# A gated MLP behind an RWKV recurrence: sequence parts of 256 tokens in place of halves of 384

## The chip, the core and the metric

The kernel runs on one core of a Trainium2 chip. TensorE (PE) multiplies, VectorE (DVE), ScalarE (ACT) and GpSimd (POOL) do the element-wise work, and SyncE (SP) issues the transfers. The metric is the device time of one execution in microseconds, as the median of several executions.

## What is computed

Four sequences of 768 tokens, 8 heads of width 48, go through a recurrence; its output, 384 wide, goes through a gated MLP that also mixes along the sequence.

```python
for t in range(S):                                     # S = 768
    cur = einsum('bhd,bhe->bhde', u[None] * kt, vt)
    y[:, :, t] = einsum('bhd,bhde->bhe', rt, state + cur)
    state = wt[..., None] * state + einsum('bhd,bhe->bhde', kt, vt)
x = y.transpose(0, 2, 1, 3).reshape(B, S, 384)
h = gelu(x @ w_in)                                     # 384 -> 1024
u, v = h[..., :512], h[..., 512:]
v_n = (v - mean(v)) / sqrt(var(v) + 1e-6) * g_ln
v_s = einsum('ts,bsd->btd', w_sg, v_n) + b_sg[None, :, None]
out = x + (u * v_s) @ w_out                            # 512 -> 384
```

The weights of w_in and w_out arrive as 64-bit numbers.

## The kernel before

The recurrence is cut into 24 chunks of 128 tokens (6 for each of the 4 sequences), called steps. A step loads decays, keys, receptances and values, scans the decays on VectorE (`decays`), and then needs PE for many products of 64x64 (`scores`, `products`, `outputs`; from the seventh step on these are one piece, `stretch`). VectorE puts the masked scores in place (`masked`, L776) before a step's outputs can be made, and forms the states between (`state`, `decayed`). A step leaves its output in the PSUM tile `y_ps` as four turned blocks of 128 columns. `taken` copies them to SBUF: two blocks and one block to `x`, the fourth to `y3`, from where three small transfers per step or half (`move`) bring rows of heads 3 and 7 into `x`. `split_x` splits `x` into two fp32r numbers, a high part `xh` and the rest `xl`.

The MLP works on halves of a sequence, `HALF` = 384 tokens (three steps). Each product of two fp32 matrices is made as three fp32r products, high by high, high by low, low by high (`mm3_part`, L976 to L978). There are four kinds of pieces, and each gathers in one PSUM bank (`m_ps`, three banks, and `resets`, a fourth from the eighth step on):

- `v_piece`, one per step (24): 9 products of 512 columns. ACT takes the GELU, ACT, POOL and DVE normalise and split the result into `vn`.
- `u_piece`, 4 per half: 9 products of 384 columns, then a GELU on ACT (L1032).
- `gate_piece`, 4 per half: 18 products of 384 columns over all six `vn` of the sequence, then a chain DVE (L1054), DVE (L1056), ACT (L1058), DVE (L1060) that leaves the gated tile `g` and frees the bank.
- `out_piece`, 3 per half: 12 products of 384 columns over the half's four `g`, an add on DVE (L1078) into one of two tiles `o`, and a transfer to `out`. The very last one is cut into two of 192 columns.

So there are 216 products of 512 columns, 1140 of 384 and 24 of 192. The sequence weights w_sg come in as 6 loads of 384 KB and are split in `f32_weight`.

A planner (`Plan`) writes the order of every engine's instructions when the program is built: each piece is a generator that yields one operation after the other with the engines it may go to, and what is next is chosen by ranks (`LEAD`, `FIRST`, `PIECE`, `WEIGHT`, `SHIFT`, `AHEAD`) and by the planner's own costs. The engines then run these orders strictly in sequence. Gaps of PE that the planner sees early in the program are filled with products that nobody reads (`warm`, L510).

Of the kernel before, what the change touches and what calls it, by code (L numbers as in the profile page):

```python
# [29 lines left out]
HALF = S // 2  # L30
NB = 2 * NP
# [5 lines left out]
LEAD = (11.6025, 5.98611, 1.71578, -0.150446)  # L37
FIRST = {"v": -3.83166, "u": 19.8393, "gate": 1.89446, "out": 11.2319}
PIECE = {"v": -2.4207, "u": 7.13579, "gate": 9.59843, "out": -5.81453}
WEIGHT = {"v": -11.5804, "u": -32.1839, "sg0": 28.8303, "sg1": -2.3904, "out": -5.37898}  # L40

BIAS = {"DVE": 0.305835, "POOL": 0.124508}
TOL = {"ACT": 0.0369713, "DVE": 0.040863, "PE": 0.0432678, "POOL": 0.0667837, "SP": 0.02}
OWN = {"ACT": 0.12, "DVE": 0.12, "PE": 0.0, "POOL": 0.1}
SHIFT = {
    "f64_weight": {3: -0.0614381, 4: 0.171028, 7: -1.58436, 8: 0.20308, 9: 1.30876},
    "f64_check": {0: -0.0471499, 1: 0.159946, 3: 0.257724, 4: 0.297904, 5: 0.297904, 6: 0.297904, 7: -0.0975631,
        8: 0.0401798, 9: 1.01451},
    "range_check": {1: -0.671107, 4: -0.273385, 5: -0.692899, 6: -1.18207, 7: 0.365565, 8: 0.257825, 9: -7.61137,
        11: -0.201453},  # L50
    "f32_weight": {0: 0.266801, 1: 0.266801, 2: 1.2626, 3: 0.777485, 4: 0.777485, 5: 0.406698},
    "columns": {0: 1.52176},
    "consts": {0: 1.1105},
    "load_v": {0: 0.477108, 2: 0.231396, 3: 0.0395037, 4: -0.138812, 5: -0.736247, 6: -1.71658, 7: -0.736247,
        8: -0.736247, 9: -0.0362696, 10: -0.620509, 11: 0.110577, 12: 0.251922, 13: 0.533938, 14: 0.0194044,
# [12 lines left out]
    "decayed": {0: -1.48561, 3: 0.136849, 4: 0.0768776, 8: -1.85101, 9: 0.25626, 13: -0.520287, 14: -0.520287,
        15: -0.520287, 16: -0.520287, 17: -0.520287, 18: -0.520287, 19: -0.0972287},
    "outputs": {1: 0.014777, 2: -1.0276, 3: 0.123273, 4: 0.123273, 5: 0.531604},  # L70
    "decays": {2: 0.0537525, 3: 0.104777, 4: -0.706109, 8: 0.360113, 11: 0.0881192, 13: 0.435941, 15: 0.223668,
        18: -1.17132, 19: 0.0148464, 20: -0.0367773, 21: 0.0148464, 23: -0.0570478},
    "masked": {2: -1.53943, 3: 0.373784, 5: -5.29511, 7: 0.0206628, 9: 0.973368, 11: 0.387743, 12: 2.10614,
        13: -2.29062, 15: -0.0676852, 17: -0.805431, 18: -0.805431},
    "taken": {2: -1.13338, 3: -0.0634019, 7: -0.898706, 11: -1.06242, 14: -0.384535, 15: -3.82209, 16: -0.589404,
        17: 0.771624, 18: -0.12312, 19: 0.0250502, 21: 4.68329, 22: 0.138749, 23: 0.0264215},
    "load_w": {4: -0.131786, 5: 0.0401692, 6: 0.0401692, 7: -0.121604, 8: 0.0401692, 9: -0.164737, 10: -0.0704624,
        12: 0.188933, 13: 0.0377871, 15: 0.902008, 17: 0.289032, 18: -0.0123312, 20: -0.246017, 21: -1.39921,
        22: 0.915889, 23: 10.1272},
    "load_rk": {0: -0.685585, 8: -0.0367111, 9: -0.0654356, 10: -0.0654356, 11: -0.0654356, 12: -0.328397,  # L80
        13: 0.156304, 14: -0.0654356, 15: -0.99069, 17: 0.197626, 18: 0.0344045, 19: 0.0344045},
    "load_kr": {6: 0.0701331, 7: -0.328212, 8: 0.0701331, 9: 0.0701331, 11: 0.123607, 13: -1.42981, 14: -1.42981,
        15: -1.42981, 18: 0.450623, 19: 0.569158, 20: 0.569158, 21: 0.118535, 22: 0.337379},
    "stretch": {0: -0.014311, 1: 3.71987, 2: -0.0649968, 3: -0.305745, 4: -0.0196869, 7: 5.17364, 9: 0.181751,
        10: 0.0035684, 11: 2.497, 12: 0.0035684, 13: 0.263689, 15: 0.0334773, 16: 0.583982},
    "chunk_pc": {7: -3.79915, 8: -2.65237, 9: -3.8422, 10: 0.110729, 19: -0.652345, 20: 0.179569, 22: 3.75926,
        23: -0.146839},
    "turned_copy": {2: -2.70266, 3: 2.36122, 5: 0.715675, 6: -3.03549, 7: 0.715675, 9: -0.172946, 10: -0.287854,
        11: -2.02959, 15: -0.298449},
    "move": {0: 1.40363, 1: -0.0424312, 2: 0.162164, 3: -0.0424312, 5: -0.771782, 6: 0.514385, 7: 0.0471732,  # L90
        8: 0.84335, 9: 0.319766, 10: 0.657144, 11: 0.040942},
    "split_x": {0: 0.10165, 1: -0.157134, 3: -3.17149, 4: -0.0132548, 5: -0.112868, 6: -0.112868, 7: 11.4787,
        8: -0.180189, 9: -9.43369, 10: 4.40471, 11: 5.72521, 12: 12.8962, 13: 0.0052103, 18: 0.523091, 21: 1.51135,
        22: 0.815484, 23: 1.22284},
    "v_piece": {1: 0.44266, 4: 0.117358, 7: 0.0515489, 8: 0.0515489, 13: -0.241269, 14: 0.172728, 15: 0.172728,
        19: -1.50804, 22: -8.36947, 23: 1.91087},
    "gate_piece": {0: 0.0381263, 2: -1.34922, 3: -0.0424933, 4: -2.33629, 8: -4.06543, 9: -4.20633, 10: -4.20633,
        11: -4.20633, 12: -4.20633, 19: 0.103656, 21: -0.533896, 25: -0.154439, 26: -2.39311, 27: -0.644318,
        28: -0.644318},
    "out_piece": {0: -5.63328, 2: -0.0987209, 3: 0.17867, 7: 3.7878, 8: 0.328413, 9: 0.328413, 10: 0.328413,  # L100
        11: 0.42777, 12: 0.42777, 13: 0.0993568, 14: 0.0993568, 15: -2.84073, 16: 3.05659, 17: -0.0251354,
        19: -0.134011, 20: 0.199046, 22: 5.16223, 23: -0.367422, 24: -2.24201},
    "u_piece": {4: 6.46487, 5: 6.1215, 6: 4.75292, 7: 5.03861, 8: 4.53855, 9: 1.98717, 11: 0.120666, 14: -0.26405,
# [294 lines left out]
def rwkv_gmlp(ctx: ExitStack, tc: tile.TileContext, wpad, kr, vtok, ktok, vt, u, ucol, w_in, consts_, w_sgT, w_out, out):  # L398
# [502 lines left out]
    def taken(n):  # L901
# [529 lines left out]
```

## Time and profile before

| | |
|---|---|
| median of 3 executions | 362.49 us (362.28 to 363.86) |
| the profiled execution, its own time | 362.22 us |
| span in its profile | 360.5 us |
| PE busy | 349.4 us, 97% of the span |
| DVE busy | 270.1 us, 75% |
| ACT busy | 201.9 us, 56% |
| POOL busy | 96.5 us, 27% |
| PE clock granted | 0.997 of full speed |
| moved by DMA | 57.06 MB, mean 158 GB/s |

The span is what the profiler records on the core; the rest of an execution's own time, 1.7 us here, lies around it. Busy shares are means over the span: PE runs through all of it, DVE is near full in the first 200 us and a third busy afterwards, when only MLP pieces are left. A product's row in the profile gives how long it is under way, from its start to the modelled end. Consecutive products overlap, so the pace of PE is read from start to start.

### The profile page before, as it was taken

Reading aid. Unit: us, or ns where it says so; the run is one execution under the profiler, and the core shown is the slowest. Engines: PE = TensorE matmul, PEld = TensorE weight load, DVE = VectorE, ACT = ScalarE, POOL = GpSimd, SP = SyncE. Lnnn points to the kernel's source line nnn. Section 1 sums busy time; section 2 is a strip of 40 time slices with the busy share of each in tenths; the row PEclk is TensorE's granted clock in tenths of the full one; section 3 lists DMA queues with packets and bytes.
Section 4 is the critical chain, followed back from the end, with each engine's and each line's share of the span. In section 5 each row is a group of like instructions: output and inputs, shape, how many; then the busy total and the mean of one; then the engine's idle time right before and its main releaser. Section 6 shows DMA issues by size and latency. Waiting matters only on the chain.

```text
span 360.5 us, 10959 instructions
## 1 busy us (share of the span) xinstructions
PE 349.4 (97%) x4507; PEld 321.5 (89%) x4507; DVE 270.1 (75%) x555; ACT 201.9 (56%) x526; POOL 96.5 (27%) x158
## 2 busy tenths in 40 slices
PE   7999999999999999999999999989999999999992
PEld 7887688899999899899999899879998989999991
DVE  6999999999999989988999979638322545362341
ACT  2847797852534655753343455835267999991110
POOL 7234444214044422226432132223000024200000
PEclk9999999999999999999999999999999999999998
DMA  7969987512448627533664234123546935521001
GB/s 249 368 197 364 318 280 233 158 32 76 162 140 254 191 82 236 171 124 122 189 220 152 79 95 139 43 82 98 163 140 202 308 99 175 188 60 65 2 11 63
DMA packets 26697, 57.06 MB, mean 158 GB/s; under 512 B 3216, under 2 KB 12176, under 8 KB 26640
## 3 DMA queue, kind: packets, MB, share of 16 engines
q1 hardware_dynamic: 26640, 56.29, 48.5%
q8 instruction: 37, 0.61, 0.7%
q14 instruction: 20, 0.16, 0.1%
HBM read 50.37 MB, written 4.72 MB: 153 GB/s over the span
## 4 chain that ended last, share of the span: by engine, by line
PE 90%; DMA 4%; POOL 2%; SPq 1%; issue 1%; DVE 0%; DVEq 0%; POOLq 0%
PE m_ps L976 18%; PE m_ps L977 18%; PE m_ps L978 18%; PE resets L976 6%; PE resets L977 5%; PE resets L978 5%; PE a_ps L699 5%; PE y_ps L722 4%; PE y_ps L733 3%; PE y_ps L706 2%; DMA RK<-in_ktok 2%; DMA x<-y 2%; PE m_ps L510 1%; PE a_ps L706 1%; DMA out<-o 1%; PE m_ps L965 1%
## 5 line engine op out<-in xcount | busy, mean ns | idle before, releaser
L976 PE MATMUL m_ps<-wsgh,vn 128*128 128x384 f32 x138 | 47.1, 341 | 0.0
L977 PE MATMUL m_ps<-wsgl,vn 128*128 128x384 f32 x138 | 46.6, 338 | 0.0
L978 PE MATMUL m_ps<-wsgh,vn 128*128 128x384 f32 x138 | 46.6, 338 | 0.0
L1007 POOL TENSOR_TENSOR st<-st,mhalf 128x1 f32<-128x1 f32 x24 | 14.0, 582 | 67.6 <-DVE st L1005 34.8
L976 PE MATMUL m_ps<-xT,winh 128*128 128x384 f32 x78 | 27.1, 348 | 0.0
L977 PE MATMUL m_ps<-xT,winh 128*128 128x384 f32 x78 | 26.4, 339 | 0.0
L978 PE MATMUL m_ps<-xT,winl 128*128 128x384 f32 x78 | 26.4, 338 | 0.0
L976 PEld LDWEIGHTS m_ps<-wsgh,vn 128*128 128x128 f32 x138 | 25.9, 188 | 0.5
L977 PEld LDWEIGHTS m_ps<-wsgl,vn 128*128 128x128 f32 x138 | 25.9, 188 | 0.2
L978 PEld LDWEIGHTS m_ps<-wsgh,vn 128*128 128x128 f32 x138 | 25.9, 188 | 0.0
L976 PE MATMUL m_ps<-g,wouth 128*128 128x384 f32 (+1 forms) x76 | 25.7, 339 | 0.0
L977 PE MATMUL m_ps<-g,wouth 128*128 128x384 f32 (+1 forms) x76 | 25.5, 335 | 0.0
L978 PE MATMUL m_ps<-g,woutl 128*128 128x384 f32 (+1 forms) x76 | 25.5, 335 | 0.0
L1054 DVE SCALAR_TENSOR_TENSOR m_ps<-m_ps,flat 128x384 f32<-128x384 f32 x23 | 14.2, 621 | 14.9 <-PE m_ps L978 14.7
L1058 ACT CAST g<-m_ps 128x384 fp32r<-128x384 f32 x23 | 10.9, 477 | 24.9 <-DVE m_ps L1056 24.9
L663 POOL TENSOR_TENSOR RK<-RK,flat 128x384 f32<-128x384 f32 x15 | 15.2, 1012 | 35.7 <-DVE W L609 11.8
L976 PE MATMUL m_ps<-winh,xT 128*128 128x512 f32 x60 | 24.7, 411 | 0.0
L978 PE MATMUL m_ps<-winh,xT 128*128 128x512 f32 x60 | 23.7, 396 | 0.0
L977 PE MATMUL m_ps<-winl,xT 128*128 128x512 f32 x60 | 23.7, 396 | 0.0
L1032 ACT ACTIVATE u<-m_ps 128x384 f32<-128x384 f32 x26 | 12.7, 493 | 19.5 <-PE m_ps L978 19.5
L405 ACT COPY x<-y_ps 128x256 f32<-128x256 f32 (+1 forms) x39 | 11.2, 328 | 22.0 <-PE y_ps L722 16.6
L722 PE MATMUL y_ps<-a,vtok 64*64 64x64 f32 x768 | 21.6, 224 | 1.3 <-issue 1.2
(194 smaller groups left out, 1031.6 us busy)
## 6 DMA issues: line engine op xcount, KB each, us to landing
KR<-in_kr SPq DMA_DIRECT2D x24, 512.0 KB, 4.8
RK<-in_ktok SPq DMA_DIRECT2D x20, 384.0 KB, 3.6
W<-in_wpad SPq DMA_DIRECT2D x24, 260.5 KB, 3.3
KR<-in_wpad SPq DMA_DIRECT2D x12, 521.0 KB, 4.4
vtok<-in_vtok SPq DMA_DIRECT2D x24, 192.0 KB, 3.3
out<-o SPq DMA_DIRECT2D x23, 192.0 KB, 2.5
vn<-in_w_in SPq DMA_DIRECT2D x6, 512.0 KB, 5.6
KR<-in_w_in SPq DMA_DIRECT2D x6, 512.0 KB, 4.1
```

What stands on the lines that cost most here:

```text
L405: nc.scalar.copy(o, i) if e == "ACT" else engine[e].tensor_copy(o, i)
L663: engine[op.e].tensor_tensor(t[:, 0], t[:, 0], u_bc, ALU.mult)
L699: nc.tensor.matmul(ps_[64 * c_:64 * c_ + 64, j, p * C:p * C + (2 * T if c_ < turn else T)], x.K[rows, at:at + T], r_, start=True, stop=True)
L706: m = behind(m, nc.tensor.matmul(at(c_)[64 * j:64 * j + 64, p // 2, p % 2], x.kt.tile[64 * c_:64 * c_ + 64, j, p * 64:(p + 1) * 64], x.V[6 ...
L722: m = nc.tensor.matmul(place(y, j, q, r, c_), x.V[64 * c_:64 * c_ + 64, h * D - up(p, j):h * D - up(p, j) + 64], x.a.tile[64 * c_:64 * c_ ...
L976: nc.tensor.matmul(ps, lh, rh, start=(i == 0), stop=False)
L977: nc.tensor.matmul(ps, lh, rl, start=False, stop=False)
L978: nc.tensor.matmul(ps, ll, rh, start=False, stop=(i == n - 1))
L1007: nc.gpsimd.tensor_tensor(rstd, var, c.mhalf, ALU.pow)
L1032: nc.scalar.activation(h_.u[f].tile, ps, AF.Gelu_apprx_tanh)
L1054: nc.vector.scalar_tensor_tensor(ps, ps, c.g[:, d:d + 1], c.b_bc[:, ts], ALU.mult, ALU.add)
L1058: nc.scalar.copy(gh, ps)
```

## The change

The MLP works on three parts of 256 tokens (`PARTS` = 3, `PART` = 256, two steps each) in place of two halves of 384.

- All fp32r products have 256 columns: u, gate and out pieces become 12 instead of 8 sets, each piece with as many products as before; a `v_piece` makes its 512 columns as two products of 256 side by side in one bank. That is 2160 products: 432 for v, 432 for u, 864 for gates, 432 for outputs.
- `taken` copies three of the four blocks in one instruction, so a step has two copies instead of three.
- The tiles for `x`, `xT`, `u`, `g` and `o` are 256 wide; there are 5, 3, 12, 4 and 2 of them (3, 2, 8, 4 and 2 before).
- The outputs of the last part go into free `u` tiles instead of the two `o` tiles, and the last output piece is no longer cut in two.
- w_sg comes as 9 loads of 256 KB.
- All ranks of the planner and its costs for the changed pieces are new, and so is the order on every engine.

```diff
+GP = 2
+PART = GP * C
+PARTS = S // PART
-LEAD = (11.6025, 5.98611, 1.71578, -0.150446)
+LEAD = (6.61435, 3.0082, 1.07907, -0.0504834)
...
-    s_x = slots("x", 3, [KT, HALF])
+    s_x = slots("x", 5, [KT, PART])
-    s_xt = homes("xT", 2)
+    s_xt = homes("xT", 3)
-    s_u = slots("u", 8, [HALF])
+    s_u = slots("u", 12, [PART])
-    s_o = slots("o", 2, [HALF])
+    s_o = slots("o", 2, [PART])
...
     def taken(n):
-        y0, y1 = (y.tile[:, j, :, 0:C] for j in range(2))
+        three = y.tile.rearrange("p j q t -> p (j q) t")[:, 0:3, 0:C]
-        copy(op.e, half.x.tile[:, 0:2, cs], y0)
-        op = yield Op({"ACT": 0.19, "DVE": 0.22}, free=[y], apart=True)
-        copy(op.e, half.x.tile[:, 2, cs], y1[:, 0])
+        copy(op.e, half.x.tile[:, :, cs], three)
         op = yield Op({"ACT": 0.19, "DVE": 0.22}, take=[s_y3] if first else [], free=[y], apart=True)
-        copy(op.e, half.y3.tile[:, cs], y1[:, 1])
+        copy(op.e, half.y3.tile[:, cs], y.tile[:, 1, 1, 0:C])
...
     def v_piece(b, g):
         for k in range(KT):
-            mm3_part(m.tile, ((xh[:, k, cs], xl[:, k, cs]),
-                              (c.win_h[:, k, FF:2 * FF], c.win_l[:, k, FF:2 * FF])), k, KT)
+            for i in range(2):
+                at, fs = (slice(o + i * FF // 2, o + (i + 1) * FF // 2) for o in (0, FF))
+                mm3_part(m.tile[:, at], ((xh[:, k, cs], xl[:, k, cs]), (c.win_h[:, k, fs], c.win_l[:, k, fs])), k, KT,
+                         i == 0, False)
...
     def u_piece(b, half, f):
-            ps = m.tile[:, :HALF]
+            ps = m.tile[:, :PART]
     def gate_piece(b, half, d):
-        ds, ts = slice(d * 128, d * 128 + 128), slice(half * HALF, (half + 1) * HALF)
+        ds, ts = slice(d * 128, d * 128 + 128), slice(half * PART, (half + 1) * PART)
-            ps = m.tile[:, :HALF]
+            ps = m.tile[:, :PART]
...
-    def out_piece(b, half, i, k=0, parts=1):
+    def out_piece(b, half, i):
-        op = yield Op({"DVE": 0.06 + 0.42 / parts}, take=[s_o], free=[m, h_.x])
+        op = yield Op({"DVE": 0.33}, take=[s_u if (b, half) == (B - 1, PARTS - 1) else s_o], free=[m, h_.x])
-        nc.vector.tensor_tensor(o.tile[:, 0:w], ps, h_.x.tile[:, i, at], ALU.add)
-        yield dma(192 // parts, free=[o])
+        nc.vector.tensor_tensor(o.tile, ps, h_.x.tile[:, i], ALU.add)
+        yield dma(128, free=[o])
...
     def f32_weight(src, hi, lo, done, after):
-        op = yield dma(384, take=[s_g], slack=2.0, after=after)
+        op = yield dma(256, take=[s_g], slack=2.0, after=after)
```

Three places show what the new order does. The first is the end of the program on VectorE: in both the rows begin with the last gate (`bad` is a one-element result that is ready there), and the rows that write `o` or `u` are the last output adds. Before:

```order
L1054 SCALAR_TENSOR_TENSOR m_ps_0_132<-m_ps_0_132,flat 128x384
L1102 TENSOR_SCALAR bad<-m_ps_0_133 1x1
L1056 TENSOR_TENSOR m_ps_0_132<-m_ps_0_132,u_0_120 128x384
L1060 TENSOR_TENSOR g_4508<-m_ps_0_132,g_4508 128x384
L1078 TENSOR_TENSOR o_0_129<-resets,x_0_111 128x192
L1078 TENSOR_TENSOR o_0_128<-m_ps_0_134,x_0_111 128x192
L1078 TENSOR_TENSOR o_0_129<-m_ps_0_133,x_0_111 128x384
L1078 TENSOR_TENSOR o_0_128<-m_ps_0_132,x_0_111 128x384
```

With the change, at the same place on VectorE:

```order
L1087 SCALAR_TENSOR_TENSOR m_ps_0_138<-m_ps_0_138,flat 128x256
L1133 TENSOR_SCALAR bad<-resets 1x1
L1089 TENSOR_TENSOR m_ps_0_138<-m_ps_0_138,u_0_130 128x256
L1093 TENSOR_TENSOR g_5457<-m_ps_0_138,g_5457 128x256
L1109 TENSOR_TENSOR u_0_121<-m_ps_0_140,x_0_111 128x256
L1109 TENSOR_TENSOR u_0_122<-m_ps_0_139,x_0_111 128x256
L1109 TENSOR_TENSOR u_0_127<-resets,x_0_111 128x256
```

Four adds that take turns in two tiles have become three adds in three tiles. The second place is PE shortly after its last gate piece: the first products of the last outputs that read the last gate tile, which is `g_4508` before and `g_5457` with the change. Before:

```order
L976 MATMUL m_ps_0_133<-g_4464,wouth 128x384
L977 MATMUL m_ps_0_133<-g_4464,wouth 128x384
L978 MATMUL m_ps_0_133<-g_4464,woutl 128x384
L976 MATMUL resets<-g_4508,wouth 128x192
L977 MATMUL resets<-g_4508,wouth 128x192
L978 MATMUL resets<-g_4508,woutl 128x192
```

With the change, on PE:

```order
L1007 MATMUL m_ps_0_139<-g_5436,wouth 128x256
L1008 MATMUL m_ps_0_139<-g_5436,wouth 128x256
L1009 MATMUL m_ps_0_139<-g_5436,woutl 128x256
L1007 MATMUL m_ps_0_140<-g_5457,wouth 128x256
L1008 MATMUL m_ps_0_140<-g_5457,wouth 128x256
L1009 MATMUL m_ps_0_140<-g_5457,woutl 128x256
```

Between the last product of the last gate and the first one that reads its tile, PE had 18 products of 192 columns and 6 of 384; now it has 18 of 256. The third place is SP's queue at about 22 us, where the first step's output rows (`x<-y`) go out among the loads; `g<-in_w_sgT` are the loads of w_sg and `RK<-in_ktok` those of a step's keys and receptances. Before:

```order
L568 DMA KR_0_83<-in_kr 128x1024
L1168 DMA g_456<-in_w_sgT 128x2x384
L582 DMA RK_0_90<-in_ktok 128x768
L1168 DMA g_488<-in_w_sgT 128x2x384
L1168 DMA g_499<-in_w_sgT 128x2x384
L582 DMA RK_0_91<-in_ktok 128x768
L576 DMA vtok_0_88<-in_vtok 128x384
L568 DMA KR_0_84<-in_kr 128x1024
L944 DMA x_0_110<-y_0_113 32x128 x3
```

With the change, on SP:

```order
L974 DMA x_0_110<-y_0_115 32x128
L615 DMA RK_0_90<-in_ktok 128x768
L615 DMA RK_0_91<-in_ktok 128x768
L1199 DMA g_505<-in_w_sgT 128x2x256
L1199 DMA g_524<-in_w_sgT 128x2x256
L1199 DMA g_532<-in_w_sgT 128x2x256
L592 DMA W_0_81<-in_wpad 128x521
L609 DMA vtok_0_88<-in_vtok 128x384
L601 DMA KR_0_84<-in_kr 128x1024
L974 DMA x_0_110<-y_0_115 32x128 x3
```

One load of 512 KB (`KR_0_83`) has gone ahead of the first step's rows, the three loads of w_sg between the first and the second step's rows are a third smaller, and a load of the decays (`W_0_81`) has come in between.

More of the change, by code (lines that the diff above doesn't have):

```diff
@@ L34 @@
 WMID, WHALF = 1.11, 0.48
-LEAD = (11.6025, 5.98611, 1.71578, -0.150446)
[L38 to L43, printed above, removed]
+LEAD = (6.61435, 3.0082, 1.07907, -0.0504834)
+FIRST = {"v": 0.538535, "u": 10.0542, "gate": 8.23501, "out": 1.251}
@@ L44 @@
+PIECE = {"v": -32.3005, "u": 3.53526, "gate": 6.48944, "out": -13.6143}
+WEIGHT = {"v": -7.69722, "u": -28.2188, "sg0": -18.159, "sg1": 0.318838, "sg2": -1.30212, "out": -26.9792}
+BIAS = {"DVE": 0.430508, "POOL": 0.254095}
+TOL = {"ACT": 0.108412, "DVE": 0.0272938, "PE": 0.107725, "POOL": 0.0671664, "SP": 0.02}
 OWN = {"ACT": 0.12, "DVE": 0.12, "PE": 0.0, "POOL": 0.1}
 SHIFT = {
-    "f64_weight": {3: -0.0614381, 4: 0.171028, 7: -1.58436, 8: 0.20308, 9: 1.30876},
-    "f64_check": {0: -0.0471499, 1: 0.159946, 3: 0.257724, 4: 0.297904, 5: 0.297904, 6: 0.297904, 7: -0.0975631,
-        8: 0.0401798, 9: 1.01451},
@@ L650, in own_weights @@
             engine[op.e].tensor_tensor(t, x.K, x.R, ALU.mult)
-            op = yield Op({"PE": 0.8}, small=True, after=[e_uc], take=[m_m], free=[rk], n=16)
+            op = yield Op({"PE": 1.0}, small=True, after=[e_uc], take=[m_m], free=[rk], n=16)
             m, = op.got
@@ L904, in taken @@
         x = ch[n]
-        half = halves[b, g // 3]
-        first = g % 3 == 0
-        cs = slice((g % 3) * C, (g % 3) * C + C)
-        op = yield Op({"ACT": 0.3, "DVE": 0.35}, after=[x.e_ym], take=[s_x] if first else [], apart=True)
+        half = halves[b, g // GP]
+        first = g % GP == 0
+        cs = slice((g % GP) * C, (g % GP) * C + C)
+        op = yield Op({"ACT": 0.42, "DVE": 0.47}, after=[x.e_ym], take=[s_x] if first else [], apart=True)
         y = x.y
-        y0, y1 = (y.tile[:, j, :, 0:C] for j in range(2))
+        three = y.tile.rearrange("p j q t -> p (j q) t")[:, 0:3, 0:C]
         y.done(op.seen)
@@ L1041, in gate_piece @@
                 first += e_wout
-            op = yield Op({"PE": 0.53}, after=[s_.e_v[s], e_wsg[s, half], *first], take=[] if s else [m_m, s_g],
+            op = yield Op({"PE": 0.347}, after=[s_.e_v[s], e_wsg[s, half], *first], take=[] if s else [m_m, s_g],
                           done=h_.e_gm[d] if s == NC - 1 else None)
@@ L1049, in gate_piece @@
             vn.done(op.seen)
-        yield Op({"DVE": 0.54}, after=[e_u, h_.e_u[d]])
-        g.n = KT + ((b, half) == (B - 1, 1))
-        g.new(2, HALF, dtype=F32R)
+        yield Op({"DVE": 0.37}, after=[e_u, h_.e_u[d]])
+        g.n = KT
+        g.new(2, PART, dtype=F32R)
         gh = g.tile[:, 0]
         nc.vector.scalar_tensor_tensor(ps, ps, c.g[:, d:d + 1], c.b_bc[:, ts], ALU.mult, ALU.add)
-        yield Op({"DVE": 0.5}, free=[h_.u[d]])
+        yield Op({"DVE": 0.35}, free=[h_.u[d]])
@@ L1082, in verdict @@
+        yield dma(128, free=[o])
+        nc.sync.dma_start(out[b, ms, half * PART:(half + 1) * PART], o.tile)
     def verdict():
@@ L1105, in rwkv_gmlp @@
     e_win = [[Event() for _ in range(KT)] for _ in range(2)]
[L1106 removed]
+    e_wsg = {(s, i): Event() for s in range(NC) for i in range(PARTS)}
     e_wout = [Event() for _ in range(FT)]
@@ L1228, in rwkv_gmlp @@
     for b in range(B):
-        for i in range(2):
+        for i in range(PARTS):
             h_ = halves[b, i]
@@ L1245, in rwkv_gmlp @@
             for m in range(KT):
-                parts = 2 if (b, i, m) == (B - 1, 1, KT - 1) else 1
-                for k in range(parts):
-                    plan.add(h_.n + at["out"] + 0.1 * m + 0.01 * k, out_piece(b, i, m, k, parts))
+                plan.add(h_.n + at["out"] + 0.1 * m, out_piece(b, i, m))
     plan.add(50.0, verdict())
```

240 lines of the change are left out of this document (128 added, 112 removed), and 13 rows, old and new, of the table SHIFT.

## The prediction

> **What bounds the kernel now.** I read three views in this order: the chain of work that ended last, what PE waited for, and the busy time of each engine by stage. The chain gives each step's share of the span; the list of PE's waits, here from 60 us on, gives engine, line, releaser, total us, times and the longest; the stages give busy us and, in brackets, instructions.
>
> ```profile
> PE 90%; DMA 4%; POOL 2%; SPq 1%; issue 1%; DVE 0%; DVEq 0%; POOLq 0%
> ```
>
> ```profile
> PE y_ps L722 <- issue: 1.2, 1, 1.2
> PE y_ps L706 <- issue: 0.2, 1, 0.2
> ```
>
> ```profile
> core 0: us, PE busy (x) PEld busy (x) DVE busy (x) ACT busy (x) POOL busy (x), PEclk, DMA share, GB/s
> 0.00:45.00 45.00, 42.58 (x674) 33.86 (x674) 41.04 (x85) 26.78 (x80) 20.63 (x49) 1.00 0.86 300
> 60.00:100.00 40.00, 40.00 (x405) 37.55 (x404) 39.51 (x86) 23.06 (x66) 9.29 (x14) 1.00 0.38 118
> 100.00:200.00 100.00, 100.00 (x1636) 94.34 (x1635) 92.26 (x177) 48.72 (x144) 36.83 (x43) 1.00 0.56 173
> 300.00:353.50 53.50, 53.42 (x309) 52.41 (x307) 23.96 (x53) 27.63 (x50) 4.56 (x8) 1.00 0.25 77
> 353.50:360.50 7.00, 0.00 (x0) 0.00 (x0) 0.56 (x1) 0.00 (x0) 0.00 (x0) 0.85 0.19 64
> ```
>
> PE carries 90% of the chain, and after the start-up it waits for next to nothing: 1.4 us in 300, and that for no other engine ("issue"). From 60 to 200 us it has no idle time at all, at the full granted clock, although DVE is nearly full beside it (131.8 of 140 us). In the first 45 us PE, DVE and DMA (0.86, 300 GB/s) share the bound, and the last 7 us belong to the end of the output. So the time is PE's work, plus the start-up, plus the end. A busy PE is not yet the pace of PE, since products overlap; the pace is read from start to start, in the timeline (start, us under way, line, tiles, shape):
>
> ```profile
> 281.08 0.34 PE L976 MATMUL m_ps<-wsgh,vn 128*128 128x384 f32 x1
> ...
> 282.47 0.34 PE L978 MATMUL m_ps<-wsgh,vn 128*128 128x384 f32 x1
> 300.13 0.34 PE L977 MATMUL m_ps<-g,wouth 128*128 128x384 f32 x1
> ...
> 301.89 0.34 PE L978 MATMUL m_ps<-g,woutl 128*128 128x384 f32 x1
> 304.19 0.39 PE L976 MATMUL m_ps<-winh,xT 128*128 128x512 f32 x1
> ...
> 305.82 0.40 PE L977 MATMUL m_ps<-winl,xT 128*128 128x512 f32 x1
> ```
>
> ```profile
> 349.50 0.27 PE L977 MATMUL resets<-g,wouth 128*128 128x192 f32 x1
> ...
> 350.06 0.36 PE L976 MATMUL m_ps<-g,wouth 128*128 128x384 f32 x1
> 7.42 0.97 PEld L655 LDWEIGHTS m_ps<-u_col,RK 128*128 128x128 f32 x8
> ```
>
> The 384-wide pace is 0.1738 us here for gates (8 products from 281.08 to 282.47) and 0.1760 for outputs (10 from 300.13 to 301.89). The 512-wide one is 0.2329 (7 from 304.19). The 192-wide one is 0.112 (5 from 349.50). The last row shows eight weight loads of 128 columns in 0.97 us under products of only 8 columns; one load is under way for 0.19, so they follow each other every 0.111. A product of 192 columns therefore pays for its weights, while those of 384 and 512 pay for their columns, at 0.453 to 0.458 ns a column.
>
> **The products, part by part.** Before, 1140 x 0.176 + 216 x 0.2329 + 24 x 0.112 = 200.6 + 50.3 + 2.7 = 253.6 us. Afterwards there are 2160 products of 256 columns, which no row shows. The columns are the same, 552,960; twice as many as need be would only hurt if a product fell under the floor of its weights. From below the bound is that floor, 0.112. From above it is the line through 384 (0.1760) and 512 (0.2329), 0.0569 for 128 columns, so 0.1760 - 0.0569 = 0.1191. By the column, 256 x 0.453 to 0.458 is 0.116 to 0.1173. I take 0.1165: the rows by the column are the nearest, and it lies in the middle of them, between the two ends. That makes 251.6 us, **2.0 us less** than before, with bounds of 241.9 (11.7 less) and 257.3 (3.7 more).
>
> [...]
>
> **The evictions on DVE and ACT.** These rows give the count, then ns as min/median/max, first and last start, and shapes:
>
> ```profile
> L1054 DVE SCALAR_TENSOR_TENSOR m_ps<-m_ps,flat x23: 609/625/627, 85.8 to 346.2; 128x384 f32<-128x384 f32 x23
> L1056 DVE TENSOR_TENSOR m_ps<-m_ps,u x23: 548/566/567, 86.9 to 346.9; 128x384 f32<-128x384 f32 x23
> L1060 DVE TENSOR_TENSOR g<-m_ps,g x23: 532/548/558, 88.4 to 348.0; 128x384 fp32r<-128x384 f32 x23
> L1078 DVE TENSOR_TENSOR o<-m_ps,x x19: 357/557/558, 105.6 to 354.5; 128x384 f32<-128x384 f32 x18, 128x192 f32<-128x192 f32 x1
> ```
>
> ```profile
> L405 ACT COPY x<-y_ps x39: 265/372/375, 21.1 to 278.0; 128x256 f32<-128x256 f32 x22, 128x128 f32<-128x128 f32 x17
> ```
>
> An add of 192 columns takes 357 ns and one of 384 takes 557, so 192 columns are worth 200 ns and the rest is fixed: 128 columns less save 0.13 us. A gate's three DVE instructions fall from 1.74 us to 1.35, but there are 48 gates instead of 32: 64.8 us for 55.6. Output adds go from 23 x 0.557 + 2 x 0.357 = 13.5 us to 36 x 0.424 = 15.3. So DVE gains 11.0 us of work. On ACT one more block costs 0.1 us, so the merged copy of three blocks costs 0.47 for 0.37 + 0.27 in two, 0.17 less for each of 24 steps, some 4 us. These 11.0 us on DVE cost the span nothing as long as PE finds its next step ready. Before, at the twentieth step, the masked scores are written 18.6 us ahead of PE's outputs:
>
> ```profile
> 213.90 0.74 DVE L776 COPY_PREDICATED a<-mask,a_ps 128x512 f32<-128x512 uint8 x1
> ...
> 233.20 0.46 PE L722 MATMUL y_ps<-a,vtok 64*64 64x64 f32 x16
> ```
>
> In the new order 54,144 fewer product columns stand ahead of that step on PE, so PE comes 54,144 x 0.455 ns = 24.6 us earlier. On DVE the instructions ahead of it add up to 12.1 us less by their own durations; as these overlap (297 us in sum, 270 busy), that is 11.0 us. Estimated spare time: 18.6 - 24.6 + 11.0 = **5.0 us**, the narrowest of the later steps. I count the evictions at zero; without that cover, every us on DVE ahead of there is a us of PE.
>
> **The gate chain.** A part's outputs need its last gate's tile. At the end of the program the chain from the last gate product to that tile is (PE, then DVE, ACT):
>
> ```profile
> 345.85 0.34 PE L978 MATMUL m_ps<-wsgh,vn 128*128 128x384 f32 x1
> 346.12 0.19 PE L1100 MATMUL m_ps<-cnt,ones 128*1 128x1 f32 x2
> 346.24 0.36 PE L976 MATMUL resets<-g,wouth 128*128 128x192 f32 x1
> ```
>
> ```profile
> 346.23 0.63 DVE L1054 SCALAR_TENSOR_TENSOR m_ps<-m_ps,flat 128x384 f32<-128x384 f32 x1 [0.86 <-PE m_ps L978]
> 348.00 0.56 DVE L1060 TENSOR_TENSOR g<-m_ps,g 128x384 fp32r<-128x384 f32 x1 [0.54 <-ACT g L1058]
> ```
>
> The product ends at 346.19 and the tile is there at 348.56, after 2.37 us. PE covers it with 18 x 0.112 + 6 x 0.176 from 346.24, until 349.31, so 0.75 us are to spare. With the change the four instructions lose 0.13, 0.13, 0.1 and 0.13, so the chain is 1.88. The cover is 18 x 0.1165, plus 0.24 for the other matmul and the last pace, less some 0.30 that the last product is still under way: 2.04. It is still covered, by 0.16 us. Cost zero, but this margin is what the slower case below turns on.
>
> **The end.** The last add and what it waits for:
>
> ```profile
> 353.08 0.33 PE L978 MATMUL m_ps<-g,woutl 128*128 128x384 f32 x1
> 354.50 0.56 DVE L1078 TENSOR_TENSOR o<-m_ps,x 128x384 f32<-128x384 f32 x1 [1.86 <-DMA out<-o]
> ```
>
> PE is done at 353.41, but the add starts only at 354.50, because its `o` tile is still being sent. In tiles of `u` nothing holds it: it starts 0.04 after the product, as at 346.23, and takes 0.42 for 0.56. From the product's end to the add's end that is 0.46 us instead of 1.65, **1.2 us less**. The transfer behind it is smaller, which I count at nothing.
>
> **The start-up.** Here the order of loads changes. Between the first and the second step's rows of x, SP issues 2,500 KB instead of 3,136; at 300 GB/s the second step's rows can land up to 2.1 us earlier. Against that, one load of 512 KB goes ahead of the first step's rows, up to 1.7 us; and on DVE the sixth step's scores come later: 5.0 us more of instructions stand ahead of them, 4.5 us with overlap, where 1.0 us was spare and PE has 5,760 more columns (2.6 us) to do meanwhile, 0.9 us lost. So between 2.1 less and 2.6 more; I take zero. PE also goes from 33 runs of products between small tiles to 35, which I leave out.
>
> **Sum.** 2.0 and 1.2 less make 3.2 less than the profiled execution's own 362.22 us (span 360.5 and 1.7 around it): **359.0 us**. That execution is 0.27 us under the median of the three runs, less than anything that is decided here.
>
> **The rivals.** *Nothing gained on the products*: they keep the pace by the column of the outputs, 0.1173, so 253.4 us, and only the end is saved; 360.8, or 364.7 at the upper bound. For it: PE is busy on columns, and these do not change. Against it: the gates at 281 us go below that pace. 22%.
>
> *Weight loads set the pace*: if streaming 256 columns hides under the 0.112 of a load, products take 241.9 us, and 11.7 + 1.2 less make 349.3. Against it: that needs 0.437 ns a column, and no row is under 0.453. [...] 11%.
>
> *The gate chain comes into the open, slower than before*: a part's last gate now has 0.16 us of spare cover, and DVE works strictly in order. Where one decay scan stands in that chain, PE waits. A scan is this row:
>
> ```profile
> L609 DVE TENSOR_TENSOR_SCAN W<-W,D 128x520 f32<-128x520 f32 x16 | 20.4, 1278 | 0.0
> ```
>
> That is 1.28 - 0.16 = 1.1 us at each part. The first seven of twelve parts lie in the stage where DVE is full, 7.8 us in all: 366.8. Before, 0.75 us and the longer pieces covered more, and PE showed no such wait. It decides once the chain in these parts is later than 0.16 us by as much as 3.2 us in all. For it: DVE is idle for only 6% of the time from 60 to 200 us. Against it: the new order can put other products there. 15%.
>
> *The start-up is late by all its bounds*, or the step at which 5.0 us are spare is missed by a little: 361 to 364. 5%.
>
> **How the numbers follow.** The forecast, 359.0, has 47%. The range leaves out most of the weight-load case and the worse half of the chain case: 353.5 to 365.5. A measurement of this kernel can tell about 0.5% from no change, 1.8 us. Faster by more than that, under 360.7: most of the forecast's share (0.40), the weight-load case (0.11) and a part of the first rival (0.05), 0.56. Slower, over 364.3: 0.18 from the chain case and the first rival's upper end. Within: 0.26.
>
> **What would show it.** In the profile of the changed kernel, products of 256 columns should start every 0.115 to 0.118 us in long runs; 0.112 or 0.119 shows a rival. PE's list of waits should have no line of gate tiles; a wait of `m_ps` products for DVE's L1093 or ACT is the chain case. The masked scores should be written at least some us before PE's outputs from the seventh step on. The last add should start within 0.1 us of the last product. The sixth step's outputs should start within 2 us of 56.2. The prediction is wrong if the pace is outside 0.112 to 0.119 or if PE shows several us of new waits.

## The result, and the profile after

| | before | changed |
|---|---|---|
| median, 4 runs each on one chip | 363.0 us (362.28 to 363.86) | 366.88 us (366.14 to 367.56) |
| ratio | | 1.0103, 95% interval 1.0073 to 1.0133 |
| profiled execution, own time | 362.22 us | 366.14 us |
| its span | 360.5 us | 364.2 us |
| last product's end, from the span's start | 353.4 us | 357.3 us |
| PE, DVE, ACT busy | 349.4, 270.1, 201.9 us | 353.0, 274.9, 217.7 us |

The change costs 1.0%. The prediction had 359.0 us, range 353.5 to 365.5: wrong side, and outside the range. The same views of the changed kernel, in the same order: the chain that ended last by engine; what PE waited for from 45 us on (total us, times, longest); busy us and, in brackets, instructions by stage.

```profile
PE 74%; DVE 11%; DMA 7%; ACT 3%; issue 2%; SPq 1%; POOL 0%; DVEq 0%; ACTq 0%; POOLq 0%
```

```profile
PE m_ps L1007 <- ACT xT L438: 0.8, 1, 0.8
PE m_ps L1007 <- ACT u L1065: 0.5, 1, 0.5
PE y_ps L766 <- ACT look L438: 0.3, 1, 0.3
PE y_ps L755 <- ACT y L438: 0.3, 1, 0.3
PE y_ps L739 <- issue: 0.2, 1, 0.2
```

```profile
core 0: us, PE busy (x) PEld busy (x) DVE busy (x) ACT busy (x) POOL busy (x), PEclk, DMA share, GB/s
45.00:60.00 15.00, 13.91 (x257) 12.63 (x250) 14.46 (x30) 13.39 (x44) 7.90 (x13) 1.00 0.86 279
60.00:100.00 40.00, 39.41 (x544) 37.38 (x543) 39.41 (x91) 21.90 (x59) 10.36 (x13) 1.00 0.40 125
100.00:200.00 100.00, 100.00 (x1963) 97.77 (x1963) 91.99 (x194) 58.90 (x178) 32.91 (x42) 1.00 0.54 164
200.00:300.00 100.00, 99.45 (x1366) 97.92 (x1365) 58.61 (x135) 76.62 (x184) 17.34 (x30) 1.00 0.55 168
357.30:364.20 6.90, 0.00 (x0) 0.00 (x0) 0.42 (x1) 0.00 (x0) 0.00 (x0) 0.82 0.15 48
```

The same stretches of the kernel before that were not shown:

```profile
45.00:60.00 15.00, 15.00 (x289) 12.03 (x289) 14.61 (x29) 12.70 (x35) 7.14 (x10) 1.00 0.77 255
200.00:300.00 100.00, 98.43 (x1203) 91.28 (x1202) 58.18 (x128) 63.01 (x156) 18.08 (x35) 1.00 0.42 132
```

From 100 to 200 us PE still has no idle time. The waits are now in the start-up: between 45 and 60 us PE is busy for 13.91 us where it was busy for all 15. No wait names a gate tile, so the gate chain stayed covered. In return the 1.2 us of PE "issue" that the list of before had at 241 us is gone. Most of the loss is not in any list of waits; it is in the pace. Outputs, then gates, from start to start:

```profile
281.00 0.28 PE L1007 MATMUL m_ps<-g,wouth 128*128 128x256 f32 x1
...
283.04 0.28 PE L1009 MATMUL m_ps<-g,woutl 128*128 128x256 f32 x1
283.15 0.28 PE L1007 MATMUL resets<-wsgh,vn 128*128 128x256 f32 x1
...
285.17 0.29 PE L1009 MATMUL resets<-wsgh,vn 128*128 128x256 f32 x1
```

The 18 outputs from 281.00 to 283.04 follow each other every 0.1200 us, the 18 gates behind them every 0.1188. Over all runs of products in the trace the means are 0.1180 for gates, 0.1177 for v, 0.1198 for u and 0.1200 for outputs: 864 x 0.1180 + 432 x (0.1177 + 0.1198 + 0.1200) = 256.4 us, **2.8 more** than the 253.6 of before, where 2.0 less was forecast. (The slow first interval of a run, 0.21 us on average in the changed kernel, is left out of these means. Read in the same way, the trace of before gives 253.7, with gates at 0.1753 and outputs at 0.1767, so its few sample rows did not mislead.) The end of the changed kernel:

```profile
357.00 0.28 PE L1009 MATMUL resets<-g,woutl 128*128 128x256 f32 x1
357.32 0.42 DVE L1109 TENSOR_TENSOR u<-resets,x 128x256 f32<-128x256 f32 x1 [1.01 <-PE resets L1009]
357.77 0.43 SPq L1111 DMA_DIRECT2D out<-u  x1
```

The last add now starts 0.04 us behind the product and ends 0.46 behind it, just as forecast (before: 1.65). Yet from the last product to the end of the span it is 6.92 us, where it was 7.09: behind the add's end it took 5.4 us before and takes 6.5 now, so 1.0 of the 1.2 us is lost again there.

The difference of 3.7 us in the span, put together from the two traces: pace of the products +2.8; waits of PE between products and the slow first product behind each, nearly all before 100 us, +2.2; PE's other products -1.2, which is the stall at 241 us; behind the last product -0.2. (Each is rounded.) That leaves three questions: why 256 columns are slow, where the 1.2 us at the end went, and what the stalls are.

### The profile page after: what moved, and what is told of

Its sections match the earlier page's. It is cut to its first block, busy times and chain, and to the rows that moved or that the text cites. A ratio compares the mean times of both kernels' runs of the same rounds, so it can differ in the third digit from the quotient of the medians.

```text
span 364.2 us, 12678 instructions
## 1 busy us (share of the span) xinstructions
PE 353.0 (97%) x5283; PEld 337.5 (93%) x5283; DVE 274.9 (75%) x608; ACT 217.7 (60%) x588; POOL 89.2 (24%) x148
## 4 chain that ended last, share of the span: by engine, by line
PE 74%; DVE 11%; DMA 7%; ACT 3%; issue 2%; SPq 1%; POOL 0%; DVEq 0%; ACTq 0%; POOLq 0%
PE m_ps L1007 16%; PE m_ps L1008 15%; PE m_ps L1009 15%; PE resets L1007 5%; PE resets L1009 5%; PE resets L1008 5%; PE a_ps L732 4%; PE y_ps L755 3%; DMA x<-y 3%; PE y_ps L766 2%; DMA KR<-in_kr 2%; PE y_ps L739 2%; DMA W<-in_wpad 1%; DMA out<-o 1%; DVE W L627 1%
## 5 line engine op out<-in xcount | busy, mean ns | idle before, releaser
L1007 PE MATMUL m_ps<-wsgh,vn 128*128 128x256 f32 x228 | 64.5, 283 | 0.0
L1008 PE MATMUL m_ps<-wsgl,vn 128*128 128x256 f32 x228 | 64.0, 281 | 0.0
L1009 PE MATMUL m_ps<-wsgh,vn 128*128 128x256 f32 x228 | 64.0, 280 | 0.0
L1007 PEld LDWEIGHTS m_ps<-wsgh,vn 128*128 128x128 f32 x228 | 43.0, 188 | 0.3
L1009 PEld LDWEIGHTS m_ps<-wsgh,vn 128*128 128x128 f32 x228 | 43.0, 189 | 0.0
L1007 PE MATMUL m_ps<-g,wouth 128*128 128x256 f32 x116 | 33.1, 286 | 0.0
L1008 PE MATMUL m_ps<-g,wouth 128*128 128x256 f32 x116 | 32.9, 284 | 0.1
L1009 PE MATMUL m_ps<-g,woutl 128*128 128x256 f32 x116 | 32.7, 282 | 0.0
L1007 PE MATMUL m_ps<-winh,xT 128*128 128x256 f32 x108 | 31.2, 289 | 0.8 <-ACT xT L438 0.8
L1007 PE MATMUL m_ps<-xT,winh 128*128 128x256 f32 x108 | 31.5, 292 | 0.5 <-ACT u L1065 0.5
L1008 PE MATMUL m_ps<-xT,winh 128*128 128x256 f32 x108 | 30.5, 283 | 0.0
L1009 PE MATMUL m_ps<-xT,winl 128*128 128x256 f32 x108 | 30.4, 282 | 0.0
L1009 PE MATMUL m_ps<-winh,xT 128*128 128x256 f32 x108 | 30.4, 281 | 0.0
L1008 PE MATMUL m_ps<-winl,xT 128*128 128x256 f32 x108 | 30.3, 280 | 0.0
L732 PE MATMUL a_ps<-KR 64*64 64x128 f32 (+1 forms) x768 | 22.4, 252 | 0.4 <-DVE S L839 0.3
```

The source lines that it names most:

```text
L732: nc.tensor.matmul(ps_[64 * c_:64 * c_ + 64, j, p * C:p * C + (2 * T if c_ < turn else T)], x.K[rows, at:at + T], r_, start=True, stop=True)
L1007: nc.tensor.matmul(ps, lh, rh, start=first and i == 0, stop=False, **shared)
L1008: nc.tensor.matmul(ps, lh, rl, start=False, stop=False, **shared)
L1009: nc.tensor.matmul(ps, ll, rh, start=False, stop=(i == n - 1), **shared)
```

## The experiments

Ratios are to the kernel before in the same set of runs on the same chip.

**The pace by itself.** A kernel of products alone, in runs of 45:

```python
for i in range(45):
    k = i // 3 % 3
    pair = ((wh, xh), (wh, xl), (wl, xh))[i % 3]
    nc.tensor.matmul(banks[s + i // 9 % 2][:, 0:w], pair[0][:, k], pair[1][:, k, 0:w], start=(i % 9 == 0), stop=(i % 9 == 8))
```

> Only fp32r products in runs of 45, each run at one width, with the three kinds of product of the kernel in turn; nothing of the reference is computed. First each width with no other engine at work, then 256, 384 and 512 with one weight tile for all, then the same three widths while VectorE runs. Theory A (a fixed cost in each product): the interval from one start to the next goes on a straight line from 256 columns up, 0.450 ns a column and 2 to 4 ns: 117 to 119 ns at 256, 175 to 177 at 384, 232 to 234 at 512, and a floor of 110 to 112 at 192 and below. Theory B (256 columns lie on the floor that loading weights sets, and neighbours disturb them): 109 to 114 ns at 256 in the quiet runs, less with one weight tile, and over 118 only in the runs with VectorE at work.

First and last product of four of the quiet runs, from the timeline:

```profile
35.31 0.28 PE L41 MATMUL bank<-xh,wh 128*128 128x240 f32 x1
...
40.23 0.27 PE L41 MATMUL bank<-xh,wl 128*128 128x240 f32 x1
40.34 0.28 PE L41 MATMUL bank<-xh,wh 128*128 128x256 f32 x1
...
45.62 0.28 PE L41 MATMUL bank<-xh,wl 128*128 128x256 f32 x1
58.26 0.34 PE L41 MATMUL bank<-xh,wh 128*128 128x384 f32 x1
...
65.89 0.33 PE L41 MATMUL bank<-xh,wl 128*128 128x384 f32 x1
75.36 0.40 PE L41 MATMUL bank<-xh,wh 128*128 128x512 f32 x1
...
85.38 0.39 PE L41 MATMUL bank<-xh,wl 128*128 128x512 f32 x1
```

Over 44 intervals that is 111.8 ns at 240 columns, 120.0 at 256, 173.4 at 384 and 227.7 at 512, all at a granted clock of 9 tenths or more. The widths of 128 to 224 gave 110.5 to 112.3; 288, 320 and 448 gave 131.7, 146.5 and 206.5. One weight tile for all products, or VectorE at work beside them, changed nothing: 119.8, 173.5 and 227.6 in both. So theory A has the shape right and the size wrong: from 256 to 384 a column costs 0.417 ns, and each product pays 13.3 ns on top (120.0 - 256 x 0.417), not 2 to 4; at 240 columns and below the floor of 110.5 to 112.3 holds. The line is not exact: 320 and 512 lie within 1 ns of it, 288 lies 1.7 ns below and 448 lies 6.4 above. Theory B falls: 256 columns take 8 ns more than the floor although nothing disturbs these products, and they are simply dearer by the column (0.469 ns) than 384 (0.452) or 512 (0.445). What the 13.3 ns are is not shown. With one weight tile the trace still has a weight load for every product (135 of each), so a cost of the load and one of the product cannot be told apart here.

**v in one product again.** In the changed kernel:

```diff
-            for i in range(2):
-                at, fs = (slice(o + i * FF // 2, o + (i + 1) * FF // 2) for o in (0, FF))
-                mm3_part(m.tile[:, at], ((xh[:, k, cs], xl[:, k, cs]), (c.win_h[:, k, fs], c.win_l[:, k, fs])), k, KT,
-                         i == 0, False)
+            mm3_part(m.tile, ((xh[:, k, cs], xl[:, k, cs]),
+                              (c.win_h[:, k, FF:2 * FF], c.win_l[:, k, FF:2 * FF])), k, KT)
```

> The changed kernel with each v product as one of 512 columns again, the order of everything else unchanged. If the pace of the products is what the change lost most by, 432 products at 117.7 ns (50.8 us) become 216 at 233.3 (50.4): 0.4 to 0.5 us less. If products of 256 columns cost nothing beyond their columns, no difference. If TensorE's instruction count matters beyond that (fewer instructions to fetch), over 1 us less.

The last product ended at 356.4 us, 0.9 earlier, but the span was 365.2 and the time 366.49 us (6 runs), ratio 1.0133 (1.0108 to 1.0158). The last three transfers' issue on SP, count and ns as min/median/max:

```profile
L1111 SPq DMA_DIRECT2D out<-u x3: 332/1227/2312, 355.1 to 357.9; - x3
```

In the changed kernel these three took 336, 384 and 431 ns. The issue of 2.3 us began at 355.5, as I read the trace while TensorE's instructions were being loaded (42 loads of 16 KB in this run); the time of that load is not on record. In the trace the 216 products follow each other every 0.2340 us, 50.5 us in place of 50.8. But a part of 0.3 or 0.4 us can't be seen in the time under such a difference, and the forecast of less time did not come; the run below with both edits takes it up.

**SP's closing instructions moved.** The program ends with a jump over a branch that is not executed here. That branch got 30 transfers more:

```diff
 def f64_weight_any(nc, pool, src, hi, lo):
...
-    nc.sync.dma_start(raw, src)
+    for i in range(4): nc.sync.dma_start(raw[32 * i:32 * i + 32], src[32 * i:32 * i + 32])
```

> The changed kernel with 30 more transfers on SP in the branch that is not executed (each weight tile's load there cut into four), so that the closing instructions stand elsewhere in SP's program; what is executed is the same. If the 1.43 us in SP's closing waits is a fetch of instructions at the edge of a block, it goes: the span falls by 1.2 to 1.5 us, and the time from the last product's end to the end of the span from 6.9 to about 5.5 us. If it is a wait for a transfer or for another engine, it stays and the span is the same.

SP's closing waits of the changed kernel, then of this run (count, ns, first and last start):

```profile
L1455 SPq EVENT_SEMAPHORE  x10: 17/28/28, 361.4 to 364.1; - x10
L1455 SPq DRAIN  x3: 7/7/7, 363.4 to 363.7; - x3
```

```profile
L1455 SPq EVENT_SEMAPHORE  x10: 17/28/28, 361.0 to 362.3; - x10
L1455 SPq DRAIN  x3: 7/7/7, 361.5 to 361.8; - x3
```

From the first of these waits to the first DRAIN it was 2.0 us, now 0.5; from the last product to the end of the span 5.34 us for 6.92. The span is 362.3, the time 364.96 us, ratio 1.0086 (1.0065 to 1.0106). What is executed is the same, only where it stands has changed. So the gap belongs to the place of the instructions, and the reading that fits is that SP waited there for its own: the changed kernel's trace has two loads of 8 KB of instructions that begin in this gap, at 361.47 and 361.68. The loads alone do not show it, since this run has such loads at 360.97 and 361.26 and no gap. The gap is 1.43 us in the changed kernel, and 1.39 and 1.35 in the runs with 512 columns and with short Squares, which leave SP's program as it is. That is where 1.0 of the 1.2 us of the end had gone.

**Both edits.**

> Both edits of the first set at once in the changed kernel: v products of 512 columns, and SP's closing instructions moved by the 30 transfers in the branch that is not executed. If all costs seen there add, the last product ends at about 356.4 us and the closing wait of 1.4 us is gone. The issue of the last two transfers took 2.3 and 1.2 us in the run with 512 columns, while TensorE's instructions were loaded: if that belongs to the place of TensorE's loads, it stays, and the span is 363.5 to 364; if it was chance, the issue takes 0.4 us and the span is 361.5 to 362.

The last product ended at 358.0, not 356.4: PE waited for 0.5, 0.9, 0.4 and 0.7 us until 42, 57, 144 and 213 us, where the run with 512 columns alone had 1.0, 0, 0.2 and 0. The issue of the transfers took 0.33 to 0.39 us again. Time 365.08 us, ratio 1.0050 (1.0030 to 1.0069). What the v products save by their pace, 0.4 us, was not seen in a time: waits of one execution differ by more. The closing wait stayed away (5.45 us from the last product to the end of the span), so that part holds in two kernels.

**Less work for ScalarE in the start-up.** The sum of squares of the first four blocks of v is taken over 64 of 512 columns:

```diff
-        nc.scalar.activation(junk[:, 0:FF], v, AF.Square, bias=neg, accum_out=var)
+        w = 64 if b == 0 and g < 4 else FF; nc.scalar.activation(junk[:, 0:w], v[:, 0:w], AF.Square, bias=neg, accum_out=var)
```

> The changed kernel with the Square over v (the sum of squares of the layer norm) for the first four blocks taken over 64 of 512 columns, the rest of that sum left out; order and everything else unchanged. If ScalarE's queue is what holds the u products back at 55.8 us (the split of x stands behind two Squares there), the wait of 0.8 us there falls under 0.2 and the last product ends 0.7 to 1.2 us earlier than 357.3. If the late transfer of the x rows (landing at 54.2) holds it, the wait keeps over 0.5 us and the end moves by less than 0.3 us.

ScalarE's timeline in the changed kernel:

```profile
54.24 0.51 ACT L438 CAST xT<-x 128x384 fp32r<-128x384 f32 x1 [1.03 <-DMA x<-y]
54.65 0.72 ACT L1036 ACTIVATE junk<-v,st 128x512 f32<-128x512 f32 x1
...
55.56 0.72 ACT L1036 ACTIVATE junk<-v,st 128x512 f32<-128x512 f32 x1
...
56.38 0.47 ACT L438 CAST xT<-m_ps 128x384 fp32r<-128x384 f32 x1
```

ScalarE first waits for the rows of x, and then two Squares stand ahead of the second half of the split, for which PE's products wait. With short Squares the second CAST came 1.39 us behind the first instead of 2.14 (54.70 and 56.09), and PE's wait of 0.8 us was gone altogether. The last product came at 357.5 all the same: this execution began 0.7 us later at the fifth step's outputs (51.5 for 50.8), and a new wait of 0.5 us turned up at 128 us. The ratio is 1.0074 (1.0056 to 1.0092). So the work that stands ahead in ScalarE's queue causes this one wait; the forecast for the end failed, and the other waits of the start-up were not taken apart.

**The end alone, in the kernel before.**

```diff
-        op = yield Op({"DVE": 0.06 + 0.42 / parts}, take=[s_o], free=[m, h_.x])
+        op = yield Op({"DVE": 0.06 + 0.42 / parts}, take=[s_u if (b, half) == (B - 1, 1) else s_o], free=[m, h_.x])
```

> The kernel before with the outputs of its last half in the tiles of u in place of the two tiles of o, as the changed kernel has them for its last part; order and work are the same. If the last addition waited for the transfer out of the o tile that it takes, the time from the last product to the last addition's end falls from 1.65 to about 0.5 us and the span by 1.0 to 1.2 us, to 359.3. If the last transfer or the fetch behind the jump ends later anyway, the span is within 0.3 us of before.

```profile
353.61 0.33 PE L978 MATMUL m_ps<-g,woutl 128*128 128x384 f32 x1
353.98 0.56 DVE L1078 TENSOR_TENSOR u<-m_ps,x 128x384 f32<-128x384 f32 x1 [1.56 <-PE m_ps L978]
```

The add no longer waits for a transfer: from the last product to the add's end it is 0.6 us instead of 1.65, and to the end of the span 6.14 us instead of 7.09. But the time is 362.47 us (12 runs) with a ratio of 1.0011 (0.9986 to 1.0036): the gain that the profile shows at the end is not in the times. Here PE ended 0.5 us later than in the first profile.

**The kernel before once more.**

> The kernel before itself, unchanged, for a second profile: how far the last product's end (353.4 us) and the time from it to the end of the span (7.1 us) differ from one execution to the next. Expected within 0.5 and 0.2 us.

Last product at 353.1, then 7.10 us: both within what was expected.

**The end and the merged copy, in the kernel before.** Beside the edit of the end above:

```diff
-        copy(op.e, half.x.tile[:, 0:2, cs], y0)
+        copy(op.e, half.x.tile[:, :, cs], y.tile.rearrange("p j q t -> p (j q) t")[:, 0:3, 0:C])
         op = yield Op({"ACT": 0.19, "DVE": 0.22}, free=[y], apart=True)
         seen = max(seen, op.seen)
-        copy(op.e, half.x.tile[:, 2, cs], y1[:, 0])
```

> The kernel before with the last half's outputs in u tiles and with one copy for the first three quarters of a turned block in place of two; every order unchanged. Theory: the copy has cover and gives nothing, ScalarE and VectorE lose 24 instructions and about 4 us of work off the path; the end gives 0.9 to 1.1 us from the last product to the end of the span, and the time falls by 0.5 to 1.1 us. Rival: the start-up waits for these copies (the x rows leave earlier by 0.2 us a block), another 0.5 us or more less.

361.86 us (12 runs), ratio 0.9971 (0.9946 to 0.9995): 0.5 to 1.1 less was expected, 1.1 came. The profile does not show the gain where it was looked for: the last product ends at 353.1 as in the repeated profile of before, the add 0.6 behind it, and then the last transfer, issued at 353.75, lands only at 357.86, 4.1 us later for 3.0 before. Its last pieces start only at 356.44, 2.7 us behind the issue, just as a load of 16 KB of instructions ends that began at 354.57. In the first profile of before they start 1.5 us behind the issue, at 356.60, and the load there ends at 356.62; in the next three runs the two times again agree to 0.02 us. So these pieces seem to wait for that load. What then closes the program starts in these runs at the later of two times: this landing, and SP's first instruction behind the jump, which stands 2.55 to 2.8 us behind the branch in the eight runs where the transfer has landed by then. So the shorter copy cannot be told from the end here; the time of both together is what is measured.

**TensorE's program moved in its blocks.** The list of waits puts the 1.2 us at 241 us down to "issue": nothing that the profile shows. Before PE's first data arrive, at 6.98 us in the first profile of before, products of one column were put in, on top of the edits of the run ahead, with 16, 32 and 48 of them. The 48 are some 96 products in the trace, and the pages count as many weight loads as products, so each is four instructions:

```diff
-    warm(full, WARM[0], m_m.free[0][1])
+    warm(full, WARM[0], m_m.free[0][1]); [nc.tensor.matmul(m_m.free[0][1][0:1, 0:1], full[:, 0:1], full[:, 0:1], start=True, stop=True) for _ in range(16)]
```

> [...] Theory (TensorE's stall of 1.2 us at 241 us is a load of its instructions that comes late): it goes or moves to another dense step; sum of stalls of TensorE over 0.3 us behind 60 us between 0 and 2.4, 1.2 less if no other place is hit. Rival (it waits for work of another engine): it stays at 241 us with 0.9 to 1.2 us.

> As the run with 16 products of one column, with 32, so 128 instructions later. Theory: the stall at 241 us is gone, and where no other step is hit the last product ends 1.0 to 1.2 us earlier than in the run without them; rival: it stays.

> As the run with 16 products of one column, with 48, so 192 instructions later. Theory: the stall at 241 us is gone or shorter, another may come at another step; rival: it stays.

PE's timeline without them, then with 16:

```profile
240.72 0.43 PE L722 MATMUL y_ps<-a,vtok 64*64 64x64 f32 x12
242.33 0.33 PE L722 MATMUL y_ps<-a,vtok 64*64 64x64 f32 x4 [1.18 <-issue]
```

```profile
240.79 0.44 PE L722 MATMUL y_ps<-a,vtok 64*64 64x64 f32 x16
241.16 0.44 PE L976 MATMUL resets<-wsgh,vn 128*128 128x384 f32 x1
```

The stall in the middle of a row of 16 small products is gone in all three. With 16 and 32 no other of over 0.3 us appears behind 60 us; the last product ends at 351.5 and 352.2 us, and the times are 361.57 (0.9957, 0.9921 to 0.9993) and 361.88 us (0.9982, 0.9952 to 1.0012). The second interval includes no change, so the gain of the stall alone is seen in the profiles and not clearly in the times. With 48 a stall of 0.58 us comes in another row of small products:

```profile
122.49 0.27 PE L733 MATMUL y_ps<-KR,S 64*64 64x64 f32 x2 [0.58 <-issue]
```

That run takes 365.26 us (1.0073, 1.0043 to 1.0103), far more than this stall explains; the last section has its profiled execution. The rival, a wait for another engine, would have stayed at 241 us. So the stall belongs to the place of TensorE's instructions in its program, and a late load of them is the reading that fits: in the first profile of before such a load begins at 240.34, just ahead of the stall. That load is over at 241.45 and the stall only at 242.79, and what fills the rest is not shown. In the repeated profile of before the stall was 0.9 us. The changed kernel happened to have none there, which hid about 1.2 us of its loss.

The blocks are seen in the traces as transfers of 16 KB on one of the profile's two queues for instructions: 37 before, with 4507 products and as many weight loads, and 43 in the changed kernel, with 5283 of each (packets, MB, share). There, up to the one at 356.51 us, they begin every 251 of these instructions on average, 108 to 380 in single cases.

```profile
q8 instruction: 43, 0.70, 0.8%
```

## Why the prediction was wrong

| term | forecast | measured | |
|---|---|---|---|
| products | -2.0 | +2.8 | pace taken 0.1165, measured 0.1187 on average |
| start-up | 0 (-2.1 to +2.6) | +2.2 | for the most part waits for ScalarE |
| the last add | -1.2 | -1.2 | as forecast |
| behind the last add | 0 | +1.0 | 1.4 lost in SP's closing instructions |
| evictions, gate chain | 0 | 0 | PE waited for neither |
| PE's stall at 241 us | not counted | -1.2 | gone with the new length of the program |

The step that failed is the sentence on the pace: "I take 0.1165: the rows by the column are the nearest, and it lies in the middle of them." Pricing by the column supposes that a product has no fixed cost, and so does the sentence that more products "would only hurt if a product fell under the floor of its weights". The two widths that the trace of before had, 384 and 512, already spoke against it: the line through them is not through zero. That line was worked out as the upper bound, 0.1191, and put aside; the measured 0.1187 lies nearly on it, outside the 0.115 to 0.118 that the forecast asked for. So of the rivals the first one came, nothing gained on the products, close to its upper bound. The 366.8 us of the chain rival lie near the measured time by luck: its cause, a wait for a gate tile, is in no list of waits. Run by itself a product of 256 columns takes even 0.1200, by the 13.3 ns on top of its columns. Cutting the same columns into 2160 products instead of 1380 pays this 780 times more, which alone would be some 10 us; in the kernel it is only 2.8, because there 384 and 512 columns run slower than by themselves (0.176 and 0.233 for 0.173 and 0.228) and 256 columns a little faster. In the kernel the line through 384 and 512 leaves some 5 ns of fixed part and not 13.3. Why, the runs do not settle.

The floor was right at 0.112 (110.5 to 112.3 ns at 128 to 240 columns in the runs of products alone; that it is the cost of the weight loads is the prediction's reading and is not shown apart), and the rival built on it fell for the reason given: 256 columns take 0.464 ns a column. The gate chain stayed covered, as forecast. The evictions' 11 us more on DVE (its busy time grew by 4.8) found their cover, as forecast, and so did PE's earlier arrival at the later steps.

The start-up's bounds held, the value did not. The profile had to show the sixth step's outputs within 2 us of 56.2; they came at 60.8, with 5,760 more columns done ahead of them. (That sign was set too tight: the prediction's own 2.6 us for these columns and 0.9 us lost already make 3.5.) Of the parts that went into the zero one was a loss of 0.9 us there; up to 100 us it became 2.2, and nothing was gained against it. The wait foreseen was one for masked scores on DVE; what came was ScalarE's queue, where the split of x stands behind other work. One wait of 0.8 us of it is shown by the run with short Squares; the rest is read from the list of waits only. The prediction had added up the new work on DVE alone and counted some 4 us less on ACT for the merged copy; ACT's busy time rose by 15.8 us.

The mechanism of the last add was right to 0.01 us (0.46 forecast, 0.46 read). That it was paid out at the end of the span was taken for granted; in the changed kernel most of it went in SP's closing instructions, and in the kernel before the landing of the last transfer can take it.

## What to carry to other kernels

Price a narrower product from two widths by a line, not by its columns: the fixed part of each product is multiplied by the number of pieces. Drawn through 384 and 512 columns, the line gave 0.1191 for 256 in the kernel, where 0.1187 came, and 0.1191 in the runs of products alone, where 0.1200 came; at 240 columns and below the floor of 110.5 to 112.3 ns took over. A list of waits shows no loss of pace, so compare intervals from start to start first. Where two versions differ by under 1%, count the stalls that no engine explains in both ("issue" in the middle of a run of like instructions, gaps in the closing waits): here they came and went with the place of the instructions in the program, and they were 1.2 and 1.4 us. The lowest ratio found has the kernel before with last outputs in u tiles, the merged copy and 16 products of one column at the start: 361.57 us, ratio 0.9957 (0.9921 to 0.9993). Its interval overlaps that of the same kernel without the 16 products (0.9946 to 0.9995).

## What the hardware showed unexpectedly

With 48 products of one column ahead of the first data, TensorE's clock was lower just behind them in the profiled execution; the row of granted clock in 40 slices of the span, with 48, then with 32 of them:

```profile
PEclk9699999999999999999999999999999999999998
```

```profile
PEclk9999999999999999999999999999999999999998
```

The second slice (9 to 18 us) has 6 tenths instead of 9 or more. From 8.5 us on the run with 48 had half the clock (the 0.50 in this row of stages) for 6.83 us:

```profile
8.50:15.33 6.83, 6.83 (x61) 6.51 (x60) 1.92 (x6) 2.18 (x9) 2.15 (x3) 0.50 0.96 378
```

The first step's outputs come 4 us later than with 32, about 1.1 of it because the 48 products themselves end only at 8.2 us (the 32 at 7.1). From the fourth step on the run is about 5 us later, and 6.5 at the last product. With 16 and 32 the profiled executions had no such slice and mean granted clocks of 0.997 and 0.996, this one 0.988; no count between 32 and 48 was tried. That the 48 products cause the lower clock is not shown. This execution is the slowest of ten (367.42 us), the others' mean granted clocks go from 0.985 to 0.998, and the one at 0.998 still took 365.53 us, so the clock is not all of the difference either.

The interval of fp32r products does not rise evenly with the width: in the runs of products alone it is flat at 110.5 to 112.3 ns from 128 to 240 columns and steps to 120.0 at 256.
